# Splitting the set-up of a state-space kernel into two chains, with angles and first norms on ScalarE

## The chip, the core and the metric

The kernel runs on one core of one Trainium2 chip. A core has TensorE (PE, matmuls into PSUM), VectorE (DVE), ScalarE (ACT), GpSimd (POOL) and SyncE (SP, which here only issues DMA transfers). Each engine works through its own instruction queue in order; semaphores tie the queues together. The metric is the device time of one execution in microseconds, as the median of several runs, and beside it stands one execution that the hardware profiler recorded.

## The reference

Four layers are applied in turn to an activation `x` of 2048 positions by 512 channels, each on the layer norm of `x` and added to it: A, B, A, B, with the same weights in both A's and both B's.

```python
# layer A: a filter in the two-dimensional spectrum
X = rfft2(x, axes=(-2, -1)) * (w_r + 1j * w_i)
y = irfft2(X, s=(S, D), axes=(-2, -1))

# layer B: a long convolution with a kernel made from a state-space model
dt = exp(log_dt)[:, None]
logdA = dt * (A_re + 1j * A_im)                     # 512 channels x 128 states
P = exp(logdA[:, :, None] * arange(L))              # 512 x 128 x 2048
K = einsum("dn,dnl,dn->dl", Cc, P, dt * Bc).real    # the kernel, 512 x 2048
y = irfft(rfft(u, 2 * L) * rfft(K, 2 * L))[:L] + u * Dskip

x = x + A(layernorm(x)); x = x + B(layernorm(x))
x = x + A(layernorm(x)); x = x + B(layernorm(x))
```

Everything is float32. `K` depends on the weights alone, so it is computed once, beside the first layer A, and both layers B use it.

## The kernel before

**Two kinds of work in the first part.** The first part of the program (`run`, L1185) interleaves layer A's first application with the making of layer B's kernel `K`.

Layer A: the input comes in eight transfers (`loads`, L459). For each of 16 blocks of positions DVE takes moments (`moments`, L480); for every four blocks `spread` (L489) makes the inverse deviations with a square root on ACT and a reciprocal on DVE. `forward_a` (L524) normalises a block (`norm`, L502: on DVE by L510, or on ACT by L508 if `spread` was told to prepare a bias as well), takes sums and differences on POOL (L534, L535), folds on DVE (L540, L541) with a small copy on ACT (L542), transforms on PE (L549 to L552) and copies out on ACT (L557). `first_a` (L645) then does the 16 groups of the spectrum, and `inv_a` (L714) the 16 inverse blocks. The tuple `NORMS` (L37) says for each of the four layer norms whether ACT does it; it is true only for the third, the second layer A.

Layer B's kernel: the exponential of `logdA * l` is split into products of small tables, so that PE can form the exponents with bf16 matmuls. For that the logarithm of the coefficient `B * C * dt`, the real part `dt * A_re` and the angles in turns are needed as factors, each split into three bf16 parts whose sum is the float32 number.

`setup_k` (L978) makes them. The data lie as 128 partitions of 512 columns (four groups of 128 states), in six rows: `an` holds A_im, A_re, B_re, B_im, C_re, C_im. In order, it multiplies the two rows of A by `dt` (L990), turns the angle into turns (L991) and takes off the nearest whole number by adding and subtracting a large constant (`turns_of`, L959: L962 to L964), once for the angle and once for 64 times it. It then forms the complex product of B and C (L998 to L1001), takes absolute values on ACT (L1002), divides by the larger of the two (reciprocal, L1006, product, L1007), forms the squared length (L1008 to L1010), its logarithm (L1011), its root (L1014), and by a second reciprocal (L1017) the half-angle tangent and the arctangent on ACT (L1019). At the end come the sum of logarithms with `log_dt` (L1020, L1021), the quadrant of the phase (L1024 to L1026) and the angle for 32 steps (L1027 to L1029). `parts` (L966) then splits: a cast to bf16 on ACT (L972), a subtraction on DVE (L974), a transfer to DRAM (L975), three times for the angle (512 columns, to `spt`) and three times for all four rows of factors at once (2048 columns, to `spe`).

`load_k` (L1035) brings the factors back, turned by the way they are read, for one of eight blocks. `exp_k` (L1052) forms exponents on PE (L1050) and takes exponentials on ACT (L1066). `unit_k` (L1070), 32 times, forms angles on PE, reduces them (L1080 to L1083) and takes sine and cosine on ACT (L1085, L1086), multiplies by the exponentials on DVE (L1093, L1094) and POOL (L1097, L1098), and multiplies the two tables on PE (L1110).

**What sets the order.** Every piece of work is a generator. A planner (`Clock`, L189) runs while the program is built: it holds a cost for each engine (`COST`, L40) and for transfers, and when each engine, buffer and datum is free by these. At every step it takes, among the pieces that could start first, the one with the lowest rank, and lets it run to its next `yield`. What a `yield` names is what the next section needs: engines, buffers from a ring (`RING0` and others, L22 on, name and number of buffers), or an event (`after`). So a section between two yields is emitted as a whole, and all that lies in it is in one place in each queue. `setup_k` has rank -99 and comes before everything it competes with; moments have -20, the forward blocks -4 to 0.5, the spectrum 6 to 24, layer B's units 0 to 31. The order on the chip is then fixed, engine by engine.

The second part (`plan_rest`, L1247) applies the first B, the second A and the second B.

Of the kernel before, what the change touches and what calls it, by code (L numbers as in the profile page):

```python
# [8 lines left out]
BF = mybir.dt.bfloat16  # L9
U32 = mybir.dt.uint32  # L10
AF = mybir.ActivationFunctionType
# [11 lines left out]
RING0 = {"an": (3072, 1), "F": (2048, 1), "W": (1024, 2), "U": (1024, 2), "k": (512, 3), "hi": (1024, 2), "hj": (256, 2), "th": (512, 1), "ld": (4, 1),  # L23
         "dt": (4, 1)}
# [12 lines left out]
NORMS = False, False, True, False  # L37
# [357 lines left out]
class Net:  # L395
# [63 lines left out]
    def loads(self):  # L459

        src = self.io["A_x"].rearrange("b (p s) d -> p (b s) d", p=128)
        self.load_n()
        self.mark("kN")
        yield self.emitted("kN")
# [484 lines left out]
    def load_n(self):  # L949
        self.ld, self.an = self.w("ld", [128, 4]), self.w("an", [128, 6, 512])  # L950
        self.nc.sync.dma_start(self.ld, self.io["kLn"])
        self.nc.sync.dma_start(self.an[:, 0:2], self.io["kN"][:, 0:2])
        self.nc.sync.dma_start(self.an[:, 2:6], self.io["kN"][:, 2:6])
# [5 lines left out]
    def turns_of(self, out, t, n, k):  # L959

        nc = self.nc
        nc.vector.tensor_scalar(k, t, float(n), MAGIC, op0=OP.mult, op1=OP.add)  # L962
        nc.vector.tensor_scalar(k, k, MAGIC, None, op0=OP.subtract)
        nc.vector.scalar_tensor_tensor(out, t, float(n), k, op0=OP.mult, op1=OP.subtract)  # L964

    def parts(self, a, shape, tag, out):  # L966

        nc = self.nc
        for p in range(3):
            yield "ACT " + tag  # L970
            hi = self.w(tag, shape).bitcast(BF)[:, :int(np.prod(shape[1:])) * 2]
            nc.scalar.copy(hi, a)  # L972
            if p < 2:
                nc.vector.tensor_tensor(a, a, hi, op=OP.subtract)  # L974
            nc.sync.dma_start(out(p), hi)  # L975
            self.drop(hi)

    def setup_k(self):  # L978


        nc = self.nc
        v = nc.vector
        yield "ACT", self.after("kN")
        an, dt = self.an, self.w("dt", [128, 4])
        F, (th, k) = self.w("F", [128, 2, 2, 512]), (self.w(t, [128, 512]) for t in ("th", "k"))
        nc.scalar.activation(dt, self.ld, AF.Exp)
        four = [128, 4, 128]
        an4 = an.rearrange("p r (c n) -> p r c n", c=4)
        for r, o in enumerate((th, F[:, 0, 1])):
            v.tensor_tensor(o.rearrange("p (c n) -> p c n", c=4), an4[:, r], dt[:, :, None].to_broadcast(four), op=OP.mult)  # L990
        v.tensor_scalar(th, th, 1 / TWO_PI, None, op0=OP.mult)  # L991
        self.turns_of(th, th, 1, k)
        self.turns_of(F[:, 0, 0], th, 64, k)
        yield "DVE"
# [7 lines left out]
        nc.scalar.activation(u, w, AF.Abs)  # L1002
        g, k2 = (self.w("k", [128, 512]) for _ in range(2))
        ln = an[:, 0:2]
        v.scalar_tensor_tensor(ln[:, 0], u[:, 0], 1e-37, u[:, 1], op0=OP.max, op1=OP.max)
        v.reciprocal(g, ln[:, 0])  # L1006
        v.tensor_tensor(u, u, g[:, None, :].to_broadcast(two), op=OP.mult)  # L1007
        nc.scalar.activation(ta, u, AF.Square)  # L1008
        v.tensor_tensor(ln[:, 1], ta[:, 0], ta[:, 1], op=OP.add)
        v.tensor_scalar(ln[:, 1], ln[:, 1], 0.5, None, op0=OP.max)  # L1010
        nc.scalar.activation(ln, ln, AF.Ln)  # L1011
        yield "DVE"

        nc.scalar.activation(k2, ln[:, 1], AF.Exp, scale=0.5)  # L1014
        v.tensor_tensor(k2, k2, u[:, 0], op=OP.add)
        v.tensor_tensor(tb[:, 0], w[:, 1], g, op=OP.mult)
        v.reciprocal(k2, k2)  # L1017
        v.tensor_tensor(tb[:, 0], tb[:, 0], k2, op=OP.mult)
        nc.scalar.activation(tb[:, 0], tb[:, 0], AF.Arctan)  # L1019
        v.scalar_tensor_tensor(ln[:, 0], ln[:, 1], 0.5, ln[:, 0], op0=OP.mult, op1=OP.add)  # L1020
        v.tensor_tensor(F[:, 1, 1].rearrange("p (c n) -> p c n", c=4), an4[:, 0],  # L1021
# [323 lines left out]
```

## Time and profile before

| | |
|---|---|
| median of three runs | 880.35 us (874.12 to 883.66) |
| the profiled execution | 880.75 us |
| its span | 878.8 us |
| PE busy | 645.9 us |
| DVE busy | 564.4 us |
| ACT busy | 427.2 us |
| POOL busy | 364.4 us |
| granted TensorE clock, mean | 0.916 |
| table loads on ACT | 26 |

A row of the profile names an engine, the line of the kernel, the operation and what it writes from what it reads (`Y` and `wk` are two large tiles that hold the rings). In a view in order of time the first two numbers are the start and the duration in microseconds; in brackets stands how long the engine had been idle before and what ended that. In a group of instructions stand the count, the busy time, the mean duration in nanoseconds and the idle time before them. In a view of one line stand the shortest, median and longest duration, and the first and last start. Busy times of PE count overlapping matmuls once.

### The profile page before, as it was taken

What the parts mean: (1) busy time and instruction counts of PE and PEld (TensorE: products, weight loads), DVE (VectorE), ACT (ScalarE), POOL (GpSimd) and SP (SyncE); (2) the same over time, 40 slices, a digit from 0 to 9 for tenths busy, and PEclk for the clock granted to TensorE, in tenths of its full rate; (3) what the DMA queues carried; (4) which work ended last, traced back from release to release, by engine and by line L of the source; (5) the groups of instructions that cost most, each with busy time, mean ns of one, the idle gap of its engine ahead of it and who ended that gap; (6) DMA issues with size and microseconds to landing.
All of it is one profiled execution on the core that took longest, in us unless ns stands there. A gap on an engine that the chain in (4) does not pass through costs nothing. (4 is left out here: it accounts for less than half of the span.)

```text
span 878.8 us, 23834 instructions
## 1 busy us (share of the span) xinstructions
PE 645.9 (73%) x10024; PEld 427.8 (49%) x10024; DVE 564.4 (64%) x1086; ACT 427.2 (49%) x806; POOL 364.4 (41%) x355
## 2 busy tenths in 40 slices
PE   0048776978999787676877776789877888569776
PEld 0046554746666443443323552578656555234555
DVE  6988776557948686992433544486876698358512
ACT  2447677487778878644334032155532455213120
POOL 0047655244536465750233124255543545058310
PEclk9999789899999897898899897799998999779989
DMA  9043004423524822279997982810661065856948
GB/s 326 31 139 105 13 13 157 140 89 122 148 80 145 287 88 72 74 225 280 252 235 192 274 309 70 192 44 1 212 210 44 2 152 138 227 160 187 249 111 225
DMA packets 86634, 132.27 MB, mean 151 GB/s; under 512 B 5660, under 2 KB 58144, under 8 KB 85888
## 3 DMA queue, kind: packets, MB, share of 16 engines
q1 hardware_dynamic: 54400, 101.39, 39.3%
q10 hardware_dynamic: 32128, 29.37, 11.8%
q8 instruction: 79, 1.29, 0.6%
q14 instruction: 27, 0.22, 0.1%
HBM read 70.04 MB, written 27.13 MB: 111 GB/s over the span
## 5 line engine op out<-in xcount | busy, mean ns | idle before, releaser
L889 POOL TENSOR_TENSOR wk<-wk 128x512 f32<-128x512 f32 x64 | 80.2, 1275 | 166.8 <-DVE wk L883 153.4
L883 DVE TENSOR_TENSOR wk<-ps,Y 128x512 f32<-128x512 f32 x128 | 79.2, 683 | 71.6 <-PE ps L812 30.0
L1097 POOL TENSOR_TENSOR Y<-wk,Y 128x1024 f32<-128x1024 f32 x32 | 76.4, 2388 | 77.9 <-ACT wk L1085 49.8
L924 PE MATMUL ps<-wk,cRbT 64*128 64x256 f32 x512 | 71.2, 423 | 25.3 <-DMA wk<-Ya 13.8
L779 PE MATMUL ps<-wk,cRb 128*32 128x256 f32 x1024 | 68.5, 407 | 15.4 <-DVE wk L510 15.4
L924 PEld LDWEIGHTS ps<-wk,cRbT 64*128 64x128 f32 x512 | 58.6, 209 | 37.8 <-issue 19.6
L930 DVE TENSOR_TENSOR x<-x,ps 128x256 f32<-128x256 f32 x64 | 24.9, 408 | 73.6 <-PE ps L924 73.4
L549 PE MATMUL ps<-cRa,wk 128*128 128x128 f32 x128 | 27.1, 295 | 57.0 <-POOL wk L534 57.0
L900 PE MATMUL ps<-wk,Y 32*32 32x256 f32 x2048 | 57.3, 400 | 14.5 <-POOL wk L889 11.4
L534 POOL TENSOR_TENSOR wk<-wk 128x256 f32<-128x256 f32 x32 | 25.6, 799 | 89.4 <-DVE wk L510 55.4
L781 ACT COPY wk<-ps 128x512 f32<-128x512 f32 x64 | 36.6, 588 | 50.1 <-PE ps L779 43.0
L779 PEld LDWEIGHTS ps<-wk,cRb 128*32 128x32 f32 x1024 | 39.8, 116 | 43.2 <-DVE wk L510 13.0
L1082 DVE SCALAR_TENSOR_TENSOR wk<-wk,ps 128x1024 f32<-128x1024 f32 x32 | 38.9, 1215 | 31.8 <-ACT wk L1080 31.7
L1050 PE MATMUL ps<-wk,Y 96*128 96x512 bf16 x128 | 42.0, 403 | 16.0 <-DVE Y L1093 6.0
L510 DVE TENSOR_SCALAR wk<-x,mv,rs 128x256 f32<-128x256 f32 (+1 forms) x80 | 41.6, 559 | 18.8 <-PE ps L779 13.5
L1110 PE MATMUL ps<-Y 128*32 128x64 f32 x2048 | 41.9, 242 | 15.9 <-POOL Y L1098 13.3
L908 ACT COPY Ya<-ps 128x256 f32<-128x256 f32 x64 | 19.2, 386 | 66.8 <-PE ps L900 49.0
L1110 PEld LDWEIGHTS ps<-Y 128*32 128x32 f32 x2048 | 36.0, 124 | 30.5 <-POOL Y L1098 17.4
L1066 ACT ACTIVATE Y<-ps 128x1024 f32<-128x1024 f32 x48 | 46.6, 1031 | 6.4 <-PE ps L1050 6.3
L549 PEld LDWEIGHTS ps<-cRa,wk 128*128 128x128 f32 x128 | 21.0, 204 | 59.0 <-POOL wk L534 57.8
L736 PE MATMUL ps<-wk,cRaT 128*128 128x512 f32 x64 | 38.5, 693 | 14.7 <-ACT wk L731 9.5
L900 PEld LDWEIGHTS ps<-wk,Y 32*32 32x32 f32 x2048 | 27.6, 105 | 43.5 <-POOL wk L889 22.4
(212 smaller groups left out, 1711.6 us busy)
## 6 DMA issues: line engine op xcount, KB each, us to landing
Y<-khat SPq DMA_DIRECT2D x24, 512.0 KB, 7.1
yk<-wk ACTq DMA_DIRECT2D x32, 256.0 KB, 2.6
wk<-Y SPq DMA_DIRECT2D x16, 512.0 KB, 4.6
wk<-Ya SPq DMA_DIRECT2D x16, 512.0 KB, 4.9
Y<-in_W_dram SPq DMA_DIRECT2D x12, 515.0 KB, 4.2
x<-in_cPa_dram SPq DMA_DIRECT2D x16, 384.0 KB, 3.5
Y<-in_cGa_dram SPq DMA_DIRECT2D x12, 384.0 KB
x<-in_W_dram SPq DMA_DIRECT2D x16, 258.0 KB, 3.6
```

The source lines that it names most:

```text
L510: self.nc.vector.tensor_scalar(xn, self.x[:, s2, d], m, r, op0=OP.subtract, op1=OP.mult)
L549: nc.tensor.matmul(o, pq[:, 0, :], self.Ra, start=True, stop=False)
L779: self.nc.tensor.matmul(p[o:o + 32, 256 * h:256 * h + 256], self.Rb[:, 2 * h + j, 32 * a:32 * a + 32], xn[s], start=True, stop=True)
L883: nc.vector.tensor_tensor(t[c][:, j], x, kh[:, j, ::-1, :] if c else kh[:, j], op=OP.mult)
L889: nc.gpsimd.tensor_tensor(Z[:, :, c], t[0][:, :, c], t[1][:, :, c], op=op)
L900: nc.tensor.matmul(v[j][h][i:i + 32], gi[o:o + 32, j, 4 + 2 * s + c, :], Z[o:o + 32, j, c, :], start=c == 0, stop=c == 1)
L924: nc.tensor.matmul(q[s], self.RbT[o, i, :], y[o, i, :], start=i == 0, stop=i == 3)
L1050: self.nc.tensor.matmul(p, f[:, c:c + 128], self.oh[:k, o:o + 512], start=True, stop=True)
L1066: nc.scalar.activation(m[:, :, 1024:] if i == 2 else m[:, i, :1024], p.rearrange("p (i m) -> p i m", i=2) if i == 2 else p, AF.Exp)
L1082: nc.vector.scalar_tensor_tensor(s, c, MAGIC, p, op0=OP.subtract, op1=OP.subtract)
L1097: nc.gpsimd.tensor_tensor(E[:, 0, :1024], c, m[:, :1024], op=OP.mult)
L1110: nc.tensor.matmul(pk[32 * j:32 * j + 32, 64 * e:64 * e + 64], E1[:, r, i, :], E2[:, r, i], start=r == 0, stop=r == 1)
```

## The change

Five things change, all in the first part.

1. `load_n` transfers B and C (four rows) ahead of A (two rows), and yields between them, so that `setup_k` may start on the first transfer.
2. The set-up becomes two pieces: `setup_k` for the product and its logarithm, rank -99, and `setup_t` for the angles and `dt * A_re`, rank -98. Both have more yields, and `parts` yields before each step on another engine. The half of the factors that `setup_t` makes is split and stored by itself, in casts of 1024 columns; the ring `hi` has four buffers of half the size, `k` four instead of three.
3. The angles are multiplied by `dt` on ACT (eight instructions of 128 columns with a scale per partition), rounded by ACT's addition of the large constant, with the sign turned round, and reduced by one DVE instruction. The sum with `log_dt` also goes to ACT (four instructions).
4. The divisor is no longer the larger component but its power of two, taken from the bits of its exponent; its inverse is a second bit operation, so the first reciprocal goes. The square is scaled by one half on ACT, and the root is doubled afterwards.
5. `NORMS[0]` is true: the 16 norms of the first layer A run on ACT, and `spread` makes the bias for them by one small DVE instruction for every four blocks.

By the built programs ACT has the same number of table loads in all: one square-root load more during the set-up, one for the exponential less behind it. The order of the first part changes throughout; that of the second part is the same but for a few instructions at its beginning.

```diff
-RING0 = {... "k": (512, 3), "hi": (1024, 2), ..., "dt": (4, 1)}
+RING0 = {... "k": (512, 4), "hi": (512, 4), ..., "dt": (4, 2)}
-NORMS = False, False, True, False
+NORMS = True, False, True, False
...
         self.nc.sync.dma_start(self.ld, self.io["kLn"])
-        self.nc.sync.dma_start(self.an[:, 0:2], self.io["kN"][:, 0:2])
-        self.nc.sync.dma_start(self.an[:, 2:6], self.io["kN"][:, 2:6])
+        for rows in (slice(2, 6), slice(0, 2)):
+            self.nc.sync.dma_start(self.an[:, rows], self.io["kN"][:, rows])
+            self.mark("kN")
+            yield self.emitted("kN")
...
+    def parts(self, a, tag, out):
+        n = a.shape[1]
         for p in range(3):
-            yield "ACT " + tag
+            yield ("+" if p else "") + "ACT " + tag
+            hi = self.w(tag, [128, n // 2]).bitcast(BF)[:, :n]
             nc.scalar.copy(hi, a)
             if p < 2:
+                yield "DVE"
                 nc.vector.tensor_tensor(a, a, hi, op=OP.subtract)
+            yield "SP"
             nc.sync.dma_start(out(p), hi)
+        self.mark("factors")
...
+    def setup_t(self):
+        yield "ACT", self.after("kN", 2)
...
+        act.activation(dt, self.ld, AF.Exp)
+        act.mul(turn, dt, -1 / TWO_PI)
+        for r, (o, b) in enumerate(((th, turn), (F[:, 0, 1], dt))):
+            for c in range(4):
+                l = slice(128 * c, 128 * c + 128)
+                act.activation(o[:, l], self.an[:, r, l], AF.Identity, scale=b[:, c:c + 1])
+        for n, o in ((1, th), (-64, F[:, 0, 0]), (-32, F[:, 1, 0])):
+            yield "ACT k k"
+            act.activation(k, th, AF.Identity, scale=float(n), bias=self.magic)
+            if n != 1:
+                act.mul(q, th, float(n))
+            yield "DVE"
+            v.scalar_tensor_tensor(o, k, MAGIC, th if n == 1 else q, op0=OP.subtract, op1=OP.subtract)
+        yield "DVE"
+        v.scalar_tensor_tensor(F[:, 1, 0], th, -0.5, F[:, 1, 0], op0=OP.mult, op1=OP.add)
+        self.mark("turns")
+        yield from self.parts(F[:, 0].rearrange("p r m -> p (r m)"), "hi", lambda p: self.spe[p, 0])
+        yield from self.parts(th, "hj", lambda p: self.spt[p])
...
     def setup_k(self):
-        yield "ACT", self.after("kN")
+        yield "DVE W W", self.after("kN", 1)
...
-        v.scalar_tensor_tensor(ln[:, 0], u[:, 0], 1e-37, u[:, 1], op0=OP.max, op1=OP.max)
-        v.reciprocal(g, ln[:, 0])
+        v.scalar_tensor_tensor(k, u[:, 0], 1e-37, u[:, 1], op0=OP.max, op1=OP.max)
+        v.tensor_scalar(ln[:, 0].bitcast(U32), k.bitcast(U32), 0x7f800000, None, op0=OP.bitwise_and)
+        v.tensor_scalar(g.bitcast(U32), ln[:, 0].bitcast(U32), 0x7f800000, None, op0=OP.bitwise_xor)
...
+        yield "DVE", self.after("turns")
+            act.activation(F[:, 1, 1, l], ln[:, 0, l], AF.Identity, bias=self.ld[:, c:c + 1])
...
+        yield from self.parts(F[:, 1].rearrange("p r m -> p (r m)"), "hi", lambda p: self.spe[p, 1])
...
-        yield "SP sq st", self.after("factors")
+        yield "SP sq st", self.after("factors", 3)
...
         yield -99, self.setup_k()
+        yield -98, self.setup_t()
```

80 lines of the change are left out of this document (36 added, 44 removed).

## The prediction

> **What bounds the kernel now.** I read the page first, then the busy time by stage, then the opening 62 us in order of time, then who holds whom in the stage behind it.
>
> ```profile
> span 878.8 us, 23834 instructions
> ...
> PE 645.9 (73%) x10024; PEld 427.8 (49%) x10024; DVE 564.4 (64%) x1086; ACT 427.2 (49%) x806; POOL 364.4 (41%) x355
> ...
> PE   0048776978999787676877776789877888569776
> ...
> DVE  6988776557948686992433544486876698358512
> ...
> GB/s 326 31 139 105 13 13 157 140 89 122 148 80 145 287 88 72 74 225 280 252 235 192 274 309 70 192 44 1 212 210 44 2 152 138 227 160 187 249 111 225
> ```
> ```profile
> spe<-Y SPq DMA_DIRECT2D x3, 512.0 KB, 2.8
> ```
>
> The span is 878.8 us of the profiled execution's 880.75, so 1.95 us lie around it. In the two rows of 40 slices (22 us each) PE does nothing in the first two slices while DVE is at six to nine tenths: TensorE waits for a set-up that runs elsewhere. The columns below are stretch, its length, then busy us of PE, weight loads, DVE, ACT and POOL.
>
> ```profile
> 0.00:57.00 57.00, 1.37 (x6) 1.37 (x7) 45.72 (x79) 19.97 (x23) 2.58 (x8) 1.00 0.46 165
> ...
> 120.00:180.00 60.00, 50.57 (x720) 36.53 (x724) 42.07 (x63) 37.82 (x50) 31.67 (x22) 0.90 0.41 125
> 180.00:240.00 60.00, 49.79 (x742) 34.65 (x730) 42.72 (x63) 45.95 (x57) 29.36 (x20) 0.97 0.37 117
> 240.00:300.00 60.00, 51.25 (x712) 34.68 (x704) 38.67 (x61) 49.16 (x61) 26.57 (x18) 0.93 0.49 161
> ```
>
> In the first 57 us DVE is busy 45.72 and PE 1.37. From 120 to 300 us PE is busy 151.6 of 180, DVE 123.5, ACT 132.9: PE leads, and the rest is waits between engines. So the opening is bound by a chain on DVE, and behind it comes a dense mix whose length does not depend on when it starts. The opening in order of time (start, duration, engine, line):
>
> ```profile
> 1.20 0.42 SPq L952 DMA_DIRECT2D Y<-in_kN_dram  x1
> ...
> 5.21 1.29 DVE L990 TENSOR_TENSOR Y<-Y 128x512 f32<-128x512 f32 x2 [4.25 <-DMA Y<-in_kN_dram]
> ...
> 7.89 0.31 ACT L517 ACTIVATE nRa<-cRa 128x128 f32<-128x128 f32 x1 [5.27 <-DMA cRa<-in_cRa_dram]
> ...
> 10.05 1.22 DVE L998 TENSOR_TENSOR Y<-Y 128x1024 f32<-128x1024 f32 x1
> ...
> 13.77 1.06 ACT L1002 ACTIVATE Y<-Y 128x1024 f32<-128x1024 f32 x1 [5.57 <-DVE Y L1001]
> 14.86 0.69 DVE L1005 SCALAR_TENSOR_TENSOR Y<-Y 128x512 f32<-128x512 f32 x1 [1.12 <-ACT Y L1002]
> ...
> 15.59 3.35 DVE L1006 RECIPROCAL Y<-Y 128x512 f32<-128x512 f32 x1
> ...
> 18.97 1.22 DVE L1007 TENSOR_TENSOR Y<-Y 128x1024 f32<-128x1024 f32 x1
> ...
> 21.30 1.28 ACT L1011 ACT_TABLE_LOAD   x1
> ...
> 22.05 0.43 DVE L1010 TENSOR_SCALAR Y<-Y 128x512 f32<-128x512 f32 x1
> 22.39 0.68 DVE L485 BATCH_NORM_STATS2 st<-x 128x6 f32<-128x512 f32 x1
> ...
> 24.97 0.63 ACT L1014 ACTIVATE Y<-Y 128x512 f32<-128x512 f32 x1
> ...
> 26.84 3.35 DVE L1017 RECIPROCAL Y<-Y 128x512 f32<-128x512 f32 x1
> ...
> 30.95 0.63 ACT L1019 ACTIVATE Y<-Y 128x512 f32<-128x512 f32 x1 [4.05 <-DVE Y L1018]
> ...
> 36.39 0.69 DVE L1029 TENSOR_TENSOR Y<-Y 128x512 f32<-128x512 f32 x1
> ...
> 42.58 1.88 ACT L972 CAST Y<-Y 128x2048 bf16<-128x2048 f32 x1
> ...
> 44.71 2.26 DVE L974 TENSOR_TENSOR Y<-Y 128x2048 f32<-128x2048 f32 x1
> ...
> 47.41 1.90 ACT L972 CAST Y<-Y 128x2048 bf16<-128x2048 f32 x1 [2.95 <-DMA spe<-Y]
> ...
> 52.20 1.90 ACT L972 CAST Y<-Y 128x2048 bf16<-128x2048 f32 x1 [2.69 <-DMA spe<-Y]
> ...
> 54.02 0.97 DVE L510 TENSOR_SCALAR wk<-x,mv,rs 128x512 f32<-128x512 f32 x2
> ...
> 54.62 0.96 POOL L534 TENSOR_TENSOR wk<-wk 128x256 f32<-128x256 f32 x1 [54.18 <-DVE wk L510]
> ...
> 56.91 0.91 SPq L1041 DMA_DIRECT2D Y<-spe  x1
> ```
>
> DVE works off both the angles (L990 to L964) and the complex product and its logarithm (L998 to L1029) in one queue until 37.1. Then three casts of 2048 columns, two subtractions and two waits for a DMA split the factors until 54.1. Only then does DVE reach layer A's first norm (54.02), POOL its first sum (54.62, idle until then), and SP, 56.91, the first load of factors back for layer B's exponentials. That is what the change touches.
>
> **The change part by part, in time.** I replay the new order with these rows, in steps from start to start: a 1024-column DVE product 1.2, 512 columns 0.65 to 0.69, a one-input DVE operation 0.43, ACT 0.63 (512) and 1.06 (1024), 0.31 for a 128-column piece (the 7.89 row), a table load 1.28, one bn_stats with its aggregate 0.8.
>
> Inputs. Rows 2 to 5 (1 MB) now load ahead of the angle rows (0.5 MB). Half a megabyte issued at 1.20 was there at 5.21; at the 326 GB/s of the first slice another half adds 1.6, so DVE starts at 6.9; all rows are in by about 7.9, where a table issued behind them had landed (the ACT row). Bounds 6.5 and 7.9.
>
> Products. Four DVE instructions take 3.7 (10.05 to 13.77): 10.6. Meanwhile ACT forms the angles in eight 128-column pieces (8 x 0.31, to 10.4), nRa and the first rounding (11.3); the absolute value then ends at 12.4, where before it ended at 14.8. The 3.35 reciprocal becomes two bit operations of 0.43, so the scaled pair is ready at 12.4 + 0.69 + 0.86 + 1.22 = 15.2 instead of 20.2: 5.0 gained. The square takes ACT to 16.3; two roundings and one scaling that were DVE's stand next on ACT (2 x 0.63), then table and logarithm (2.3), table and exponential (1.9): 21.9 against 25.6. DVE has five bn_stats in between and comes at 22.9; the second reciprocal stays, so the arctangent ends at 28.2 (before 31.6), and the last factor at 32.2 instead of 37.1, because the roundings by 64 and 32 lie ahead of it. So 4.9 are gained here. What does that cost on ACT? Twelve 128-column pieces and five roundings, some 7 us, nearly all of it while DVE works; without that cover they would be 7 us on the chain. One more square-root table load (1.28) lies under the reciprocal.
>
> Splits. Before, 17.0 us from 37.1 to 54.1. Now the angle half is split while the other half is computed, in casts of 1024 (1.06). Each cast still waits until the part before it has landed (2.8 us by the DMA row above, its last column), but there is other work in that time. Behind 32.2: subtraction 34.6, second cast behind the DMA 37.3, five bn_stats on DVE to 38.6, subtraction 39.8, third cast 41.3; the small angle parts behind it end at 45.1, as DVE has three more bn_stats ahead of the last subtraction. So 12.9 instead of 17.0, and nine issues on SP instead of six, none of which another transfer waits for. Bounds: 17.0 if the waits add up as before (the end at 49.2), and 6.4 less than my 12.9 if none of the eight bn_stats stood in the way.
>
> Sum of the opening: the first norm at 45.1 instead of 54.0, the first load at 48.0 instead of 56.9. **8.9 us earlier, with bounds 4.9 and 15.3.**
>
> Layer A's first forward pass. Sixteen norms leave DVE for ACT, with four tiny biases. Busy time by group from 54 to 97 us, ACT, DVE and POOL in turn, and then the same norm on ACT in the second layer A:
>
> ```profile
> 54.00:97.00 43.00, 35.59 (x276) 29.67 (x276) 35.27 (x62) 25.92 (x49) 32.77 (x36) 0.89 0.33 101
> ```
> ```profile
> L510 DVE TENSOR_SCALAR wk<-x,mv,rs 128x512 f32<-128x512 f32 x16 | 11.3, 716 | 0.0
> L541 DVE TENSOR_TENSOR wk<-wk 128x127 f32<-128x127 f32 x16 | 9.3, 579 | 0.0
> ```
> ```profile
> L534 POOL TENSOR_TENSOR wk<-wk 128x256 f32<-128x256 f32 x16 | 13.4, 835 | 61.7 <-DVE wk L510 55.4 <-PE ps L552 3.8 <-PE ps L550 1.1
> ```
> ```profile
> L508 ACT ACTIVATE wk<-x,nb,rs x16: 797/814/816, 565.7 to 597.7; 128x512 f32<-128x512 f32 x16
> ```
> ```profile
> L557 ACT COPY Ya<-ps x16: 575/586/698, 58.7 to 96.2; 128x512 f32<-128x512 f32 x16
> ```
> ```profile
> L1110 PE MATMUL ps<-Y x2048: 216/219/317, 91.4 to 378.1; 128*32 128x64 f32 x187
> ```
>
> The pass ran 42.8 us, from 54.0 to the end of the copy that starts at 96.2. DVE was busy 35.3 and ACT 25.9 of 43. Taking off 11.3 leaves DVE 24; 16 x 0.81 = 13.0 brings ACT to 38.9, less the 0.4 that two set-up instructions left in that window: 38.5. PE has 35.6. So DVE stops being the tightest engine and ACT takes its place, in order, with layer B's exponentials queued behind the norms, and layer B's first unit (L1110, 91.4) waits for those. The pass should last about as long as before: ACT's 38.5 plus some waits at its start, where each norm goes through POOL, DVE and PE before ACT has a copy to make, against 42.8. I take 0 for it, with bounds of 4.3 us gained (ACT never idle) and 18.2 lost (rival three, the whole shift and a unit).
>
> Behind it, the order on PE keeps its sequence nearly: the first of the 32 products comes after 36 factor matmuls in both, the last with 16 inverse transforms of layer A ahead of it instead of 15. From 120 to 300 us PE leads, so the start moves the end one for one. The second part of the program, from layer B's first application on, has the same order in both but for a few instructions.
>
> Sum: 880.75 - 8.9 + 0 = 871.8 us. The profiled execution is 0.4 above the median of 880.35 (874.12 to 883.66), so no correction.
>
> The Trainium skill, ScalarE: Activation LUTs, Rules for kernel authors, speaks against the last step: it gives additions and multiplications to VectorE, as the faster engine. The rows agree on the single instruction (814 ns on ACT; two in 0.97 us on DVE in the 54.02 row, 716 ns in the mean). By that rule the norms are 16 x 0.33 = 5.3 us dearer at most, and the sum would be 877.1 if they all lay on the path.
>
> **The rivals.** One: ACT takes it back. In the second pass the norms on ACT start between 565.7 and 597.7, one per 2.13 us, with hardly any other work on ACT. With the rest of ACT's work of the first pass in the same queue (25.9 less 0.4 and less the 16 copies of 0.586, so 16.1) and 3 for the last forward's way, the pass would last 15 x 2.13 + 16.1 + 3 = 51.1 and end at 96.2 instead of 96.8: 880.1. For it: ACT works in order, and each norm needs a buffer that POOL frees. Against it: the second pass is fed by layer B's end, not by ACT.
>
> Two: more than the opening is gained. DVE and POOL disturb each other in this pass: the norm means 716 ns, L541 579 and the POOL sum 835. With the norms off DVE, ACT's 38.5 could be the whole pass: 4.3 less than 42.8, and 867.5. For it: POOL is busy 32.8 of 43 and its first sums start on the norm. Against it: L540 and L541 stay on DVE and meet the same sums. The Trainium skill, SBUF — State Buffer, Who interferes with whom, states this: a DVE operation in a two-port mode, or with two inputs in SBUF, and a GpSimd operation lock one pair of ports against each other. By that rule the norm's part of the lock goes, and L541's stays; the trace's stretched means agree.
>
> Three, slower: layer B's units fall a unit behind. Their 32 products run from 91.4 to 378.1, one per 9.25 us, each behind an ACT sine in the order of that queue. If the sixteen norms push the first product not to the 82.5 that the shift gives but beyond 91.4, the shift is gone, and a unit lost makes 880.75 + 9.25 = 890.0. It decides if the first L1110 comes later than 91.4. For it: in the new order all sixteen norms precede the first sine on ACT; against it: the shift leaves 9 us for 13 us of norms that ACT can do while it was idle (17 of 43).
>
> **How the numbers follow.** Forecast (869 to 876) 0.40; rival one (876 to 884) 0.22; rival two (860 to 869) 0.24; rival three 0.14. The range leaves out the tenth at either end: 861 to 886, which holds the bound of 4.9 for the opening (875.9) and takes in the far one (15.3, 865.4) and rival two, though not both at once (861.1 is just inside). About 1% is what a measurement of this kernel can tell from no change: below 871.5 or above 889.2 against the median. Faster than that are rival two and half of the forecast, 0.24 + 0.21 = 0.45; slower is most of rival three, 0.12; the same 0.43.
>
> **What would show it.** In the profile after: the first absolute value near 11.3, the second reciprocal starting near 23.6, the last factor near 32, the first norm on ACT at 45 and the first POOL sum at 46, the first factor load at 48, the last forward copy near 87 and the first L1110 product between 82 and 86 (under other line numbers). The last product, at 378.1 before, should lie at 369, and everything behind it as long as it was. I am wrong in the opening if DVE, in order, holds the first subtraction behind a bn_stats whose input has not landed; wrong in the pass if ACT is busy over nine tenths and the first product comes after 88; wrong in carrying it over if the last product's shift is not that of the first.

## The result: slower by 0.6%, and the profile after

The changed kernel takes 885.69 us (median of 20 runs, 879.87 to 900.55) where the kernel before took 880.68 beside it (20 runs, 874.12 to 887.02). The ratio is 1.0062, with a 95% interval of 1.0033 to 1.0092. Ratios here and below leave out executions that are more than 1.5% above the fastest of their kernel; medians take in all. Forecast was 871.8 us, 1% faster. The profiled execution of the changed kernel took 890.31 us, 4.6 above its median; its span is 888.5, so times late in its trace are some microseconds late for the kernel as a whole.

The page of the changed kernel: span, busy times, and PE and DVE in 40 slices.

```profile
span 888.5 us, 23908 instructions
...
PE 663.2 (75%) x10024; PEld 433.4 (49%) x10024; DVE 541.7 (61%) x1067; ACT 445.3 (50%) x843; POOL 362.0 (41%) x355
...
PE   0087888998887686646877786789877888477876
...
DVE  6936768567475567972433554486876698366612
```

PE's third slice stands at eight tenths instead of four, and up to the thirteenth none is below seven. The 14th to 19th (289 to 422 us) have 6, 8, 6, 6, 4, 6 where before they had 7, 8, 7, 6, 7, 6. The opening in order of time, in the changed kernel's lines (L1015 to L1057 is `setup_k`, L984 to L1001 `setup_t`, L966 and L969 the splits):

```profile
6.46 1.23 DVE L1015 TENSOR_TENSOR Y<-Y 128x1024 f32<-128x1024 f32 x1 [5.51 <-DMA Y<-in_kN_dram]
...
11.04 1.05 ACT L1020 ACTIVATE Y<-Y 128x1024 f32<-128x1024 f32 x1
...
23.08 3.35 DVE L1043 RECIPROCAL Y<-Y 128x512 f32<-128x512 f32 x1
...
30.88 0.69 DVE L1057 TENSOR_TENSOR Y<-Y 128x512 f32<-128x512 f32 x1
...
42.97 0.62 ACT L966 CAST Y<-Y 128x512 bf16<-128x512 f32 x1 [1.07 <-DVE Y L969]
...
43.50 1.52 ACT L506 ACTIVATE wk<-x,nb,rs 128x512 f32<-128x512 f32 x2
...
44.12 0.91 SPq L1067 DMA_DIRECT2D Y<-spe  x1
44.39 0.72 POOL L532 TENSOR_TENSOR wk<-wk 128x256 f32<-128x256 f32 x1 [43.95 <-ACT wk L506]
```

The first absolute value starts at 11.04 (13.77 before), the second reciprocal at 23.08 (26.84), the last factor is done at 31.57 (37.1), the first norm starts at 43.50 (54.02), the first load of factors at 44.12 (56.91). The opening is 10.5 us shorter. The pass behind it, from the first norm to the end of the last copy, by the line of those copies in the changed kernel (shortest, median, longest in ns, first and last start):

```profile
L555 ACT COPY Ya<-ps x16: 564/587/628, 48.8 to 82.0; 128x512 f32<-128x512 f32 x16
```

The line of the products of layer B's kernel in the same trace:

```profile
L1136 PE MATMUL ps<-Y x2048: 216/219/317, 82.3 to 384.5; 128*32 128x64 f32 x187
```

The last copy starts at 82.0 and ends at 82.6, so the pass takes 39.1 us instead of 42.8, and the first product comes at 82.3 instead of 91.4. All that was to be gained is there at 82 us. The last product, however, starts at 384.5 instead of 378.1. Where it went is told by the busy times up to 280 us and from there to 400 (stretch, length, busy us of PE, weight loads, DVE, ACT, POOL, then the granted clock), first of the kernel before:

```profile
0.00:280.00 280.00, 189.98 (x2465) 138.38 (x2466) 206.18 (x326) 180.37 (x239) 121.16 (x98) 0.94 0.37 117
280.00:400.00 120.00, 88.95 (x1529) 49.85 (x1535) 91.83 (x168) 83.61 (x126) 69.76 (x67) 0.87 0.48 151
```

The same view of the changed kernel:

```profile
0.00:280.00 280.00, 201.29 (x2576) 141.37 (x2576) 187.22 (x318) 211.49 (x289) 123.20 (x101) 0.93 0.38 122
280.00:400.00 120.00, 80.34 (x1325) 43.52 (x1325) 87.47 (x153) 66.04 (x105) 65.14 (x64) 0.81 0.43 138
```

At 280 us PE of the changed kernel has worked 201.3 us instead of 190.0: it is 11.3 us ahead. From 280 to 400 us it works 80.3 instead of 89.0, at a clock of 0.81 instead of 0.87, and no other engine is nearer to full (DVE 87.5 instead of 91.8, ACT 66.0 instead of 83.6). The lead goes there, and not in waits alone. The same view, up to the start of layer B's first transform (the table below has it), of the kernel before:

```profile
0.00:384.03 384.03, 263.58 (x3759) 178.97 (x3759) 286.69 (x463) 255.82 (x347) 188.61 (x161) 0.92 0.38 123
```

And of the changed kernel:

```profile
0.00:394.87 394.87, 276.51 (x3824) 182.00 (x3824) 272.98 (x465) 276.35 (x392) 188.35 (x164) 0.90 0.40 129
```

PE idles 118.4 us instead of 120.5: the idle time that the opening saved came back in the tail. Besides, PE is busy 12.9 us longer, with 3824 matmuls instead of 3759 and a granted clock of 0.90 instead of 0.92. Behind that point both traces take about as long to the end (493.6 and 494.8 us).

| (us, end of the work unless it says start) | before | after |
|---|---|---|
| unit 17's sine | 231.8 | 203.4 |
| group 15, the last of the spectrum | 289.4 | 287.8 |
| first inverse block | 308.8 | 311.8 |
| unit 31's sine | 371.8 | 378.7 |
| last inverse block | 393.3 | 392.9 |
| layer B's first transform, start | 384.0 | 394.9 |

The three strands (units, layer A's inverse blocks, layer B's first transforms) that share this tail stand in another order in the queues: the planner chose another one. The sines of units 28 and 29, and of 30 and 31, used to end as pairs (344.7 and 348.5, 367.4 and 371.8); now they end one at a time between inverse blocks (335.6, 351.4, 355.0, 378.7), and all of layer B's transforms stand behind the last block. Executions of kernels that share an order up to there put group 15 between 280.6 and 288.2, so below distances within one trace count more than times across traces.

### The profile page after: what moved, and what is told of

It reads as the page before. It is cut to its first block, busy times and chain, and to the rows that moved or that the text cites. A ratio compares the mean times of both kernels' runs of the same rounds, so it can differ in the third digit from the quotient of the medians.

```text
span 888.5 us, 23908 instructions
## 1 busy us (share of the span) xinstructions
PE 663.2 (75%) x10024; PEld 433.4 (49%) x10024; DVE 541.7 (61%) x1067; ACT 445.3 (50%) x843; POOL 362.0 (41%) x355
## 5 line engine op out<-in xcount | busy, mean ns | idle before, releaser
L1123 POOL TENSOR_TENSOR Y<-wk,Y 128x1024 f32<-128x1024 f32 x32 | 76.9, 2402 | 60.5 <-issue 30.0
L1076 PE MATMUL ps<-wk,Y 96*128 96x512 bf16 x128 | 44.2, 417 | 23.4 <-DVE Y L1119 16.0
L1108 DVE SCALAR_TENSOR_TENSOR wk<-wk,ps 128x1024 f32<-128x1024 f32 x32 | 38.9, 1215 | 36.0 <-ACT wk L1106 36.0
L1119 DVE TENSOR_TENSOR Y<-ps,Y 128x1024 f32<-128x1024 f32 x32 | 39.0, 1219 | 14.9 <-ACT ps L1112 14.8
L508 DVE TENSOR_SCALAR wk<-x,mv,rs 128x256 f32<-128x256 f32 x64 | 28.8, 494 | 28.2 <-PE ps L777 21.2
## 6 DMA issues: line engine op xcount, KB each, us to landing
x<-in_cPa_dram SPq DMA_DIRECT2D x16, 384.0 KB, 3.2
Y<-in_cGa_dram SPq DMA_DIRECT2D x12, 384.0 KB, 3.1
```

Source lines behind the costliest of these rows:

```text
L1076: self.nc.tensor.matmul(p, f[:, c:c + 128], self.oh[:k, o:o + 512], start=True, stop=True)
L1108: nc.vector.scalar_tensor_tensor(s, c, MAGIC, p, op0=OP.subtract, op1=OP.subtract)
L1119: nc.vector.tensor_tensor(E[:, 1, :1024], p, m[:, :1024], op=OP.mult)
L1123: nc.gpsimd.tensor_tensor(E[:, 0, :1024], c, m[:, :1024], op=OP.mult)
```

## The experiments

**The theory and its rivals.** Theory: the change itself gains what the opening shows, and the order that the planner made of it loses more. Rivals: the norms cost on ScalarE by themselves; and the earlier work only spends the full-speed clock earlier, so that a lower clock behind takes it back.

| run | what it is | us, median | ratio to before, 95% |
|---|---|---|---|
| e1 | changed kernel, old order | 872.2 | 0.9925, 0.9894 to 0.9956 |
| e2 | the same, norms on DVE | 874.3 | 0.9915, 0.9878 to 0.9952 |
| e3 | old set-up, norms on ACT, new order | 894.9 | 1.0160, 1.0120 to 1.0200 |
| e4 | changed kernel, norms on DVE, planner free | 876.0 | 0.9933, 0.9898 to 0.9968 |
| e5 | new order to unit 16, then old | 865.2 | 0.9820, 0.9784 to 0.9857 |
| e12 | new order to unit 22, then old | 865.1 | 0.9802, 0.9760 to 0.9843 |
| e7 | new order to unit 26, then old | 869.0 | 0.9895, 0.9857 to 0.9934 |
| e11 | new order to unit 29, then old | 876.5 | 0.9953, 0.9913 to 0.9994 |
| e6 | old order to unit 16, then new | 907.7 | 1.0302, 1.0262 to 1.0343 |
| e8 | old order to unit 26, then new | 914.2 | 1.0358, 1.0306 to 1.0410 |
| e9 | changed kernel, one rank of the plan 30 for 25 | 874.8 | 0.9918, 0.9885 to 0.9951 |
| e10 | kernel before, norms on ACT, planner free | 878.2 | 0.9967, 0.9937 to 0.9998 |
| e13 | new order, units 30 and 31 forward | 882.4 | 1.0003, 0.9972 to 1.0034 |
| e14 | new order, first two inverse blocks forward | 892.3 | 1.0124, 1.0071 to 1.0177 |
| e15 | new order, layer B's first transforms forward | 880.7 | 0.9968, 0.9931 to 1.0006 |
| e16 | e13, e14 and e15 together | 885.2 | 1.0037, 1.0004 to 1.0069 |
| e17 | e13 and e15 together | 874.3 | 0.9913, 0.9869 to 0.9957 |

**Change and order taken apart.** In these kernels the planner's choice is replaced by a written list of sections, taken from a build of one kernel and mapped to the pieces of the other; it holds from the end of the set-up on, and a section that cannot start yet is passed over for the next one that can.

```diff
-            now = min(t for t, _ in ready) + NEAR
-            t, p = min((e for e in ready if e[0] <= now), key=lambda e: e[1][:2])
...
+            if todo:
+                able = {p[1]: (t, p) for t, p in ready}
+                at = next(n for n, i in enumerate(todo) if i in able)
...
+                t, p = able[todo.pop(at)]
+            else:
+                now = min(t for t, _ in ready) + NEAR
+                t, p = min((e for e in ready if e[0] <= now), key=lambda e: e[1][:2])
```

By the traces, PE's 10024 matmuls and POOL's 355 instructions stand in e1 and e2 in the order of the kernel before (by operation, tiles and shapes), and in e3 in that of the changed kernel, but for four matmuls near 533 us.

e1 is the changed kernel with the list of the kernel before:

> The changed kernel with its whole set-up and the norms on ACT, but every piece of work behind the set-up is emitted in the order of the kernel before (its list of pieces is written into the file), so that PE and POOL have exactly the sequence of before. Theory one, the order: the opening's 10.5 us are real and were given back by the planner's new order of the dense stage; then this is some 10 us faster than before, 870 us, and the last product L1110 lands near 368 instead of 378.1. Theory two, the clock: the granted TensorE clock takes back whatever starts earlier, in any order; then 880 to 886, with a mean clock about 0.90 and the last product near 378. Theory three, the norms on ACT: they hold layer B's functions back in ACT's queue; then 876 to 886, with the first product gained and lost again before the sixteenth group.

e2 has `NORMS = False, False, True, False` besides:

> As the run with the old order, but the first norms stay on DVE as before: the set-up alone, in the order of before. The order theory: 870 to 872. The clock theory: 880 to 886. The theory of the norms: 870, and clearly faster than the run with the norms on ACT.

e3 is the kernel before with `NORMS = True, False, True, False` and the changed kernel's list:

> The kernel before, with its own set-up (one chain on DVE) but the norms on ACT and every piece behind the set-up in the order of the changed kernel; PE and POOL have exactly the changed kernel's sequence. The order theory: the loss without the gain, 885.7 + 10.5 = 896 us. The clock theory: 881 to 886, as the late start is paid back too. The theory of the norms: 890 to 896 as well, so this run tells only the clock from the other two.

e4 is the changed kernel with the old `NORMS` and no list:

> The changed kernel with the first norms back on DVE, and the planner free to choose the order anew. The theory of the norms: the loss goes, 870 to 876. The order theory: a third order, whose worth nobody can read from the list; anything from 865 to 895, with the same opening. The clock theory: 880 to 886.

With the old order the change gains: 872.2 us. With the new order the old set-up loses: 894.9. The difference between the two orders is 13.5 us behind the new set-up (885.7 against 872.2). The order theory stands. Norms on ScalarE cost nothing that can be seen under one order (e1 and e2 have nearly the same interval, each of some 6 us), and for the clock see e7 below. e4's 876.0 fits the theory of the norms as well as that of the order; e1 and e2 tell the two apart.

e10 is the fourth corner, the kernel before with the new `NORMS` and the planner free:

> The kernel before with the first layer A's norms on ScalarE and nothing else, the planner free: the fourth corner of set-up by norms (before 880, new set-up alone 876, both 885.7). The order on TensorE at the end of the first part is that of the kernel before. Theory (the order in the tail decides, the place of the norms does not): within 5 us of 880. Rival one (norms on ScalarE cost by themselves, in this set-up at least): 885 or more. Rival two (they free VectorE and gain): below 875.

With the planner free in all four, norms alone give 878.2, set-up alone 876.0, both 885.7. In the two single steps the last of the first part keeps the old pattern on PE; only with both does the planner turn it over.

**Where the new order loses.** The lists are spliced: one order until a unit begins, the other for all sections that remain. The edit is written here in short; the files hold the lists as numbers.

```diff
-ORDER[0] = new
+ORDER[0] = new[:begins(unit)] + remaining(old)      # e5, e12, e7, e11: unit 16, 22, 26, 29
+ORDER[0] = old[:begins(unit)] + remaining(new)      # e6, e8: unit 16, 26
```

> The changed kernel, in the new order until layer B's unit 16 begins (near 195 us), and from there what is left in the old order. If the loss sits behind unit 16 (theory: middle or tail), this keeps the lead that the new order has there, and ends at 870 or earlier, down to 860. If the first half does the harm (it uses up the pieces that fill waits later), it stays at 880 to 886.

> The reverse: the old order until unit 16 begins, then what is left in the new order. If the loss sits behind unit 16: 880 to 886. If in the first half: 870.

> The changed kernel, in the new order until unit 26 begins (near 285 us), then the old order. If the loss lies in the tail, where six units and sixteen inverse blocks end together: 870 to 874. If it lies in the middle, between units 16 and 26, where the lead of 20 us went: 880 to 886.

> The reverse: the old order until unit 26 begins, then the new order's tail. Tail theory: 882 to 886, with the last product some 10 us later than in the run with the old order throughout. Middle theory: 870 to 873.

> The changed kernel in its own order until unit 29 of layer B's kernel begins, and the old order for what remains. The change to the old order at unit 26 measured 869.0, none 885.7. If the loss arises in units 29 to 31 (the pairs at the very end), this stays near 869 to 874; if it is spread over units 26 to 31 evenly, 876 to 879; if it arises already in units 26 to 28, 881 to 886.

> The changed kernel in its own order until unit 22 begins, the old order behind it. The cuts at 16 and 26 measured 865.2 and 869.0. If the new order is good until 16 and harmless between 16 and 26, 864 to 870 and the last product between 357 and 363 us. If the two measured so only by the particular seam, this one falls outside, above 874.

New first and old behind is better than either order alone where the change comes at unit 16 or 22 (865.2 and 865.1); old first and new behind is worse than either. So the new order is good until unit 22 (7.1 us better than the old order throughout) and bad behind unit 26: 869.0, 876.5 and 885.7 us with the old order from unit 26 on, from 29 on, and never. The 16.7 us fall into 7.6 for units 26 to 28 and 9.1 for what follows; a difference between two such medians is uncertain by some 4 to 5 us (0.3 to 0.4% for each ratio), so the split is rough. The two reverse runs missed both of their answers: e6 gave 907.7 and e8 914.2, where at most 886 was expected. So the price of the new tail depends on what stands ahead of it: 16.7 us behind the new first part (e7), some 40 behind the old one (e8 against e1). Why it is so dear there stays open. The clock rival falls with e7, busy times up to 280 us and from there to 400:

```profile
0.00:280.00 280.00, 201.35 (x2593) 141.51 (x2593) 192.12 (x322) 214.25 (x293) 128.22 (x103) 0.94 0.39 124
280.00:400.00 120.00, 89.64 (x1549) 50.87 (x1552) 84.85 (x165) 73.12 (x119) 61.51 (x62) 0.87 0.56 168
```

Its PE has worked as much by 280 us as that of the changed kernel (201.4 and 201.3), and behind it is granted 0.87, as before, and works 89.6 us instead of 80.3. This execution is the fastest of e7's six (863.27 us, their median is 868.98), but e17 below, profiled at its median, shows the same: 201.2 us by 280 us, then 89.3 at 0.88. Early work is not paid back by the clock. The clock does go with the order: the median over the executions is 0.90 for the changed kernel (20) and 0.92 for it under the old order (e1, 12) and for the kernel before beside that (27). How much of the order's price is waiting, and how much the matmuls at that lower clock, no run separates.

e9 alters the plan by one number and leaves the planner free:

```diff
-RANK = -4, 0.3, 6, 1.2, 25, 0.5, 24, 0.5
+RANK = -4, 0.3, 6, 1.2, 30, 0.5, 24, 0.5
```

> The changed kernel with one number of the plan altered: the rank of layer A's 16 inverse blocks goes from 25 to 30, and the planner is free. On TensorE the order is that of the changed kernel up to unit 26 of layer B's kernel; behind it the remaining factor matmuls come in runs of 8 and 4 ahead of the inverse blocks instead of one unit at a time between them. If the loss lies in units 26 to 31 being held apart by inverse blocks (theory), the last product comes by 370 us (384.5 in the changed kernel, 361.9 in the run that changes to the old order at unit 26) and the time is 868 to 878. If the loss is in the tail's total work on VectorE, whichever way it is ordered (rival one), the inverse blocks are only late instead, the part behind the last product is longer by as much, and the time stays at 883 to 889.

It gave 874.8 us. The last product starts at 348.3 and layer B's first transform at 358.7, both some 36 us earlier than in the changed kernel, while the last inverse block ends at 394.0, as late as there (392.9). This agrees with late units and late transforms costing time even where the inverse blocks get no earlier, but does not show it alone: e9 also has three table loads fewer (23 instead of 26). The theory's time came, though by another end of the tail than it named.

**Which waits.** Two places in the changed kernel's trace. First unit 31, in order of time on ACT (L1106 is its rounding, L1111 and L1112 its sines):

```profile
355.89 1.15 ACT L1106 ACTIVATE wk<-ps,magic 128x1024 f32<-128x1024 f32 x1
...
375.31 1.28 ACT L1111 ACT_TABLE_LOAD   x1
376.61 1.15 ACT L1111 ACTIVATE wk<-wk,quarter 128x1024 f32<-128x1024 f32 x1
377.66 1.01 ACT L1112 ACTIVATE ps<-wk 128x1024 f32<-128x1024 f32 x1
```

The same stretch on DVE (L745 to L755 belong to inverse blocks, L1108 is the unit's reduction):

```profile
357.27 1.50 DVE L755 TENSOR_TENSOR x<-x,wk 128x256 f32<-128x256 f32 x1
...
362.27 1.35 DVE L746 TENSOR_TENSOR wk<-wk 128x127 f32<-128x127 f32 x1
...
366.03 1.48 DVE L755 TENSOR_TENSOR x<-x,wk 128x256 f32<-128x256 f32 x1
...
372.32 1.20 DVE L1108 SCALAR_TENSOR_TENSOR wk<-wk,ps 128x1024 f32<-128x1024 f32 x1
...
375.70 0.41 DVE L755 TENSOR_TENSOR x<-x,wk 128x256 f32<-128x256 f32 x1
```

The rounding is done at 357.0, the reduction starts at 372.3. In between DVE works without a gap, on inverse blocks above all (moments, copies and unit 30's products as well), several of their instructions stretched (L755 takes 0.41 us at 375.70 and 1.50 at 357.27); then the sines need a table load of 1.28 first. Second, the matmuls of PE behind the last inverse block, with the idle time in brackets:

```profile
380.92 2.07 PE L734 MATMUL ps<-wk,cRaT 128*128 128x512 f32 x2 [5.32 <-ACT wk L729]
...
394.87 3.55 PE L777 MATMUL ps<-wk,cRb 128*32 128x256 f32 x30 [9.07 <-DVE wk L508]
```

PE idles 9.07 us until the first norm of layer B (DVE, L508), which stands in DVE's queue behind all 16 inverse blocks; in the kernel before, PE began them at 384.0 and had one inverse block's second matmul still behind them. e13, e15 and e14 move these sections, and those of the first two inverse blocks, in the changed kernel's list; everything else keeps its place.

```diff
-ORDER[0] = new
+ORDER[0] = forward(new, units=(30, 31))             # e13, 10 sections
+ORDER[0] = forward(new, inverse=(0, 1))             # e14, 13 sections
+ORDER[0] = forward(new, transforms=(0, 1, 2))       # e15, 7 sections
+ORDER[0] = forward(new, all of these)               # e16
+ORDER[0] = forward(new, units and transforms)       # e17
```

This too is written in short; the files hold the lists.

> The changed kernel in its own order, but ten sections of units 30 and 31 of layer B's kernel stand earlier in the list (unit 31's reduction directly behind its rounding and one inverse block's step, its sines, products and copy behind that, unit 30's last four sections likewise); the inverse blocks keep their order. Two table loads of the tail go. If the loss comes from the last units standing behind inverse blocks in the queues (theory), the last product comes about 16 us earlier, at 365 to 371 us instead of 384.5, the last inverse block stays within 3 us of 392.9, and the time falls to 874 to 881, towards the 874.75 of the run with the altered rank. If the units' lateness is harmless because the last inverse block sets the end (rival one), the product comes earlier and the time stays at 883 to 888. If the inverse blocks are pushed back as far as the units come forward (rival two), the last of them comes after 398 and the time is 886 or more.

> The changed kernel's order with thirteen sections of the first two inverse blocks moved ahead of units 26 and 27, of two turns and of spectra; nothing else is moved. If the late first inverse block is the larger part of the loss, the first inverse block ends 8 to 14 us earlier than in the changed kernel (311.8), the last some 5 us earlier (392.9), and the time is 875 to 881. If the blocks behind it are held by something else, the first comes earlier, the last stays at 390 to 394, and the time at 883 to 888.

> The changed kernel's order with seven sections of layer B's first three transforms moved ahead of the last inverse blocks' steps on VectorE and ScalarE. If the idle 9 us of TensorE ahead of the first transform are lost time, the first transform starts 4 to 9 us earlier than 394.9 and the time is 879 to 883. If the stage behind is bound by transfers or by the later transforms, it starts earlier and the time stays at 884 to 888.

> The three moves together (units 30 and 31, the first two inverse blocks, the first three transforms of layer B). If the loss in the tail is the sum of these three, 867 to 874, where the old order from unit 26 on gave 869.0. If they are only different ends of one chain, so that one alone gives what all give, no better than the best of the three.

> The changed kernel's order with the ten sections of units 30 and 31 and the seven of layer B's first three transforms moved forward, and the inverse blocks left where they are. If the two add up (3.3 and 5.0 us from 885.7), 875 to 879, close to the 876.5 of the old order from unit 29 on. If they are one wait seen at two ends, 880 to 883.

e13 falls between its two answers (881 and 883). The last unit's sine ends at 363.8 instead of 378.7, and the time is 882.4, 3.3 us less; the last product comes at 375.4, not by 371, and two table loads of 1.28 us are gone as well (24 instead of 26). Unit 31 is a part, not the whole. e15 does what was expected; its first transforms on PE:

```profile
386.18 0.62 PE L854 MATMUL ps<-wk,cRb 128*32 128x256 f32 x4 [1.02 <-DVE wk L585]
387.45 1.92 PE L854 MATMUL ps<-wk,cRb 128*32 128x256 f32 x28 [0.65 <-DVE wk L585]
```

They start at 386.2 instead of 394.9, and the time is 880.7, 5.0 less. e17 has both, with the last product at 370.1 and the first transform at 379.0: 874.3, 11.4 less, so the two add up (8.3 singly; by the ratios 1.5% singly and 1.5% together) and cover the 9.1 us lost behind unit 29. Its busy times from 280 to 400 us are near those of the kernel before again, PE 89.3 instead of 80.3:

```profile
280.00:400.00 120.00, 89.29 (x1556) 49.13 (x1553) 86.19 (x162) 69.46 (x116) 60.80 (x62) 0.88 0.52 158
```

A third reading, that the late first inverse block costs time, found no support. In the changed kernel that block's copies and sums stand behind units and spectra on ACT and POOL. ACT of the changed kernel (L709 is the last copy of the spectrum, L729 the first of an inverse block):

```profile
287.23 0.59 ACT L709 COPY Ya<-ps 128x512 f32<-128x512 f32 x1 [1.79 <-PE ps L706]
...
298.26 1.06 ACT L729 COPY wk<-ps 128x512 f32<-128x512 f32 x2
```

POOL of the same kernel (L1123 belongs to unit 27, L742 is the block's first sum):

```profile
305.19 2.35 POOL L1123 TENSOR_TENSOR Y<-wk,Y 128x1024 f32<-128x1024 f32 x1 [4.07 <-issue]
...
308.72 0.50 POOL L742 TENSOR_TENSOR wk<-wk 128x128 f32<-128x128 f32 x1
```

ACT of e7, the same two copies:

```profile
282.08 0.59 ACT L786 COPY Ya<-ps 128x512 f32<-128x512 f32 x1 [1.79 <-PE ps L783]
284.20 0.59 ACT L806 COPY wk<-ps 128x512 f32<-128x512 f32 x1 [1.53 <-PE ps L802]
```

And the first sum on POOL of e7:

```profile
287.44 0.46 POOL L819 TENSOR_TENSOR wk<-wk 128x128 f32<-128x128 f32 x1 [5.99 <-DMA x<-in_A_x_dram]
```

So the first sum comes 21.5 us behind the last copy of the spectrum, in e7 5.4. But moving the first two blocks forward did not help: in e14 the first is done at 302.7 instead of 311.8, the last at 391.9 as before, and the time is 892.3, 6.7 more and outside both answers (875 to 881, 883 to 888); put on top of e17 it costs 10.9 (e16). What it pushes back is seen: unit 26's sine ends 15.2 us behind the last group in e14 and 14.9 in e16, 10.5 in the changed kernel and 10.0 in e17. Why that costs so much, and which of the other moves of the old order between units 26 and 28 is worth its 7.6 us, stays open; the old list also puts the turns and the spectra of layer B's kernel back there, and that was not tried alone.

## Why the prediction was wrong

**The opening: right, and too small.** The working gave 8.9 us, with bounds 4.9 and 15.3; it measured 10.5. Four marks lie within 0.7 us of the working (first absolute value 11.3 and 11.04, second reciprocal 23.6 and 23.08, last factor 32.2 and 31.57, inputs 6.9 and 6.46). Of the 1.6 us that were missed, 0.6 lie ahead of the last factor and 0.9 in the splits: 12.9 us from the last factor to the end of the last cast were forecast, 12.0 came (31.57 to 43.59).

**The pass: near the gaining bound, by the order.** Taken was 0, with 4.3 as its bound; 3.7 came. The cover that was named held: ACT takes all norms and is busy 35.6 us of the 39.1, over the nine tenths that the prediction named as a sign of being wrong here, and yet the first product was not late. The busy times of that stretch in the changed kernel:

```profile
43.50:82.60 39.10, 31.19 (x226) 26.57 (x230) 18.88 (x47) 35.59 (x65) 27.37 (x35) 0.98 0.35 101
```

But this gain belongs to the new order, not to the norms. e1 has the same set-up and the same norms on ACT in the old order; its first two norms, and the line of its copies:

```profile
43.30 1.51 ACT L582 ACTIVATE wk<-x,nb,rs 128x512 f32<-128x512 f32 x2
```
```profile
L631 ACT COPY Ya<-ps x16: 574/586/682, 48.1 to 89.6; 128x512 f32<-128x512 f32 x16
```

There the pass ends at 90.1 and takes 46.8 us, 4.0 more than before; with the norms on DVE (e2) it takes 42.2 (44.8 to 87.0).

**The step that failed** is the last one, "the order on PE keeps its sequence nearly", and with it "From 120 to 300 us PE leads, so the start moves the end one for one". The second sentence holds up to 280 us: the lead was 10.5 us at the first norm and is 11.3 us of PE's work there. It fails behind that: the first product came 9.1 us earlier and the last 6.4 later, which is the sign that the prediction had named for this step. The comparison of the orders looked at two places of PE's queue, the first product and the last; both hardly moved (16 inverse transforms ahead of the last instead of 15), and what lay between on DVE, ACT and POOL was not costed at all. That order costs 13.5 us against the old one (e1), and 16.7 in its tail alone (e7). Of those 16.7, 9.1 are traced to the last units and layer B's first transforms standing behind inverse blocks (e17); for the other 7.6 the cause stays open. With the old order the sum of the prediction comes near, 871.8 forecast and 872.2 measured (e1), but in part by luck: there the opening gains 10.7 us instead of 8.9, and the pass loses 4.0 instead of nothing. By its ratio e1 gains 6.6 us (3.9 to 9.3).

**The rivals.** Three had the sign but not the mechanism: its condition was a first product later than 91.4, and it came at 82.3; units did fall back, but the last ones, 300 us later, and not by one unit but by an order. So it is luck that 885.7 still lies in the range (861 to 886), whose upper end rests on that rival. One, ACT takes it back, did not come in this order; under the old order it has the direction right and the size too large (46.8 us in e1, 51.1 in its sum). Two, more than the opening, was true of the pass in this order, and the mutual disturbance of DVE and POOL that it named did fall. Groups of that stretch in e4, with the norms on DVE, by one of POOL's sums and one of DVE's folds (busy us and mean ns stand ahead of the idle time):

```profile
L532 POOL TENSOR_TENSOR wk<-wk 128x256 f32<-128x256 f32 x16 | 12.9, 806 | 54.0 <-DVE wk L508 46.6 <-PE ps L550 5.4 <-PE ps L548 1.4
...
L539 DVE TENSOR_TENSOR wk<-wk 128x127 f32<-128x127 f32 x16 | 9.2, 578 | 0.0
```

The same groups of the changed kernel, with its norm on ACT:

```profile
L506 ACT ACTIVATE wk<-x,nb,rs 128x512 f32<-128x512 f32 x16 | 12.9, 825 | 0.0
...
L532 POOL TENSOR_TENSOR wk<-wk 128x256 f32<-128x256 f32 x16 | 11.8, 739 | 52.2 <-ACT wk L506 44.1 <-PE ps L548 2.4 <-ACT wk L540 2.4
...
L539 DVE TENSOR_TENSOR wk<-wk 128x127 f32<-128x127 f32 x16 | 6.1, 382 | 0.0
```

The folds take 382 ns instead of 578 and the sums 739 instead of 806; under one order (e1 against e2) the same groups take 449 instead of 579 and 737 instead of 801. That this shortened the pass is not shown, since e1's pass is the longer one. The Trainium skill, SBUF — State Buffer, Who interferes with whom, says that such DVE and GpSimd work locks one pair of ports against each other, and these rows agree; the prediction had expected the folds to stay stretched as they meet the same sums, and they do so only in part. The Trainium skill's rule against the norms on ScalarE (ScalarE: Activation LUTs, Rules for kernel authors) would have cost up to 5.3 us by the prediction's estimate; the single instruction is dearer (825 ns here, 716 before), and no run shows a cost in the whole: e1 and e2 differ by it alone and have nearly the same interval.

## What to carry to other kernels

Where a planner orders the work from its own costs, an edit is two changes, the instructions and the order that follows; cost the second by itself, or hold it fixed. Here the instructions gained 0.75% (e1) and the order took 1.4% (ratio 1.0062 against 0.9925). Compare the two builds in every queue of the stage where several strands end together, not at the first and last instruction of one engine; and try the found gain with the old order before the edit is given up: new order up to unit 22 and old behind it runs at 865.1 us, ratio 0.9802 (0.9760 to 0.9843), faster than both kernels.

## What was not expected of the hardware

Moving 16 norms from DVE to ACT shortened what stayed on DVE and POOL: the folds by a third and the sums by 8% in the rows above, by 22% and 8% under one order (e1 and e2). And a table load stands alone: the square-root load at 22.49 us of the changed kernel takes 1.28 us and its activation starts at 23.79, 1.30 behind the load's start, so no further wait of ACT is seen there. The two rows in the changed kernel's order of time:

```profile
22.49 1.28 ACT L491 ACT_TABLE_LOAD   x1
...
23.79 0.30 ACT L491 ACTIVATE rs<-mv,eps 128x4 f32<-128x4 f32 x1
```
